# Attention in blocks of one token tile and sixteen heads, the first FFN layer of chunk 0 by token tiles, and the second chunk's transposes by DMA

## The chip, the cores and the metric

The kernel runs on one core of one Trainium2 chip. The metric is the device time of one execution in microseconds (us); lower is better. The time before is 501.07 us, the median of three runs (501.04 to 501.58).

## What is computed

One transformer layer over 2048 tokens of width 576: an attention with a compressive memory, then an FFN with a hidden width of 4608, each on a layer-normalized input and each with a residual.

```python
h = x + A(layernorm(x));  out = h + B(layernorm(h))

def A(x):                                  # 32 heads of 18, 4 segments of 512 tokens
    q, k, v = x @ wq, x @ wk, x @ wv
    M = z = 0;  g = sigmoid(beta)          # per head: M is 18 x 18, z is 18
    for s in range(4):
        p = softmax(qs @ ks.T * 18**-0.5 + causal_mask)
        a_mem = (phi(qs) @ M) / (phi(qs) @ z + 1e-6)   # phi(t) = t+1 if t>0 else exp(t)
        o_s = g * a_mem + (1 - g) * (p @ vs)
        M += phi(ks).T @ vs;  z += phi(ks).sum()
    return o @ wo

def B(x): return gelu(x @ w1 + b1) @ w2 + b2
```

## The kernel before

**Tiling.** A token tile is 128 tokens; a chunk is two tiles (256 tokens), so there are 16 tiles and 8 chunks (`NCH`); two chunks make a segment. All operands of matmuls are bf16. A group `g` is four heads (`G` = 8 groups): their Q and K lie transposed in `QTs` and `KTs`, one head in each quarter of the 128 partitions.

**An order planned at build.** Nothing is issued directly. Every piece of work is an `op` with an engine, a modelled duration, the keys it reads and writes, and a due time (`now` + a `SLACK` value). A small model of the engines runs through them: for ScalarE (ACT), VectorE (DVE), GpSimd (POOL) and the DMA-issuing SyncE (SP) the ready op with the earliest due time goes next (line 757); TensorE (PE) takes whichever generator ("stream") can go on, in an order of preference (lines 764 and 765). `transfer` and `begin` model one DMA queue by its rate. At the end (lines 792 to 794) all ops are issued in the order of their modelled start, which is then fixed. Each engine works its queue in that order, and waits where the chip is later than the model.

**The streams.** `stream_P(tl)` (two of them, one for each tile of a chunk) does layernorm, the transposes of the normalized tile, the Q/K/V projection (four pieces of 432 columns at lines 294 and 295), and the transposes of Q and K. For chunks below `TP` = 2 the transposes are matmuls into PSUM with copies out (lines 320 and 358, 401 and 404); from chunk 2 on they are DMA transposes on SP's queue (`dma_t`, line 130). It then makes phi(k) for the memory. `stream_M` sums phi(k)^T v (line 439). `stream_A` is the attention. `stream_B(tl)` is the output projection, the residual, the second layernorm and its transposes (matmuls for chunk 0 alone, `TB` = 1). `stream_F1` and `stream_F2` are the two FFN layers of a chunk.

**Attention.** A visit of `stream_A` is one group of four heads with up to two key tiles, for both query tiles of the chunk: `scores` puts 8 matmuls (line 482; four row groups of 32 side by side, 256 or 128 columns) into the four PSUM banks of `st4`, one exp on ScalarE takes them to `pt` (line 488; 384 or 512 columns in each bank), and an affine select on GpSimd masks each diagonal piece (line 492). `weighted` multiplies them with V (line 507, 128x19 matmuls into the PSUM bank `ox`). A chunk has 8 visits (even) or 16 (odd). The scores of a visit stand ahead of the weighted sums of the visit before it; at the end of a chunk the last sums follow with nothing ahead of them. After two groups, `finish` normalizes `ox` on VectorE (lines 547 to 560) for both tiles and eight heads; from chunk 2 on `memory_in` and `memory_mm` add the memory's part. The stream starts on a chunk when both of its tiles are projected (`done_P`), and `stream_B` when all visits of the chunk are done (`done_A`).

**FFN.** F1 of a chunk starts when both tiles have left `stream_B` (`done_B`): 9 weight groups of 512 hidden columns, each 4 x 5 matmuls of 256 columns (lines 294 and 295), with an eviction on VectorE for two of the four (line 703), and gelu on ScalarE in place over 18 hidden tiles at a time (line 711). The weight groups 0 to 4 of chunk 0 have buffers of their own (two, and three in the second hidden buffer, which is not used yet). Their loads 2 to 4 and those of W2 (`load_w2`, in the list `later`) are queued one at each attention visit. F2 (line 737) needs the gelu of the whole chunk.

**Filler.** As long as no F1 work has been issued, a TensorE that would stand idle multiplies the zeros of `pq` (line 775); the result is not read.

Of the kernel before, what the change touches and what calls it, by code (L numbers as in the profile page):

```python
# [16 lines left out]
def kernel(  # L17
# [447 lines left out]
    oxv = ox[:, 0:304].rearrange("p (u a b c) -> p u a b c", u=2, a=2, b=4)  # L465

    def scores(c, g, pieces, slot):
        s0 = c - c % 2
        placed = []
        off = 0  # L470
        for kt in pieces:
            lo = max(kt - 2 * (c % 2), 0)
            placed.append((kt, lo, off))
            off += (2 - lo) * P
        keys = [("QT", c % 2, 0), ("QT", c % 2, 1)] + [("KT", (s0 + kt // 2) % 3, kt % 2) for kt in pieces]
        sk = [("st", i) for i in range(4)]

        def go():
            for kt, lo, o in placed:
                for i in range(4):  # L480
                    rows = slice(32 * i, 32 * i + 32)
                    nc.tensor.matmul(out=st4[:, i, o:o + (2 - lo) * P],  # L482
                                     lhsT=KTs[(s0 + kt // 2) % 3][rows, g, (kt % 2) * P:(kt % 2 + 1) * P],
                                     rhs=QTs[c % 2][rows, g, lo * P:Q], start=True, stop=True, tile_position=(32 * i, 0))
# [2 lines left out]
        op("PE", 0.21 + off * MM, go, keys, sk)
        op("ACT", 0.18 + 4 * off * 0.00083, lambda: nc.scalar.activation(out=pt[:, :, 0:off], in_=st4[:, :, 0:off],  # L488
                                                                       func=ACT.Exp, scale=scale), sk, [("pt", slot)], slack=SLACK["exp"], table="exp")
        for kt, lo, o in placed:  # L490
            if kt >= 2 * (c % 2):
                op("POOL", 0.675, lambda o=o: nc.gpsimd.affine_select(  # L492
                    out=pt[:, :, o:o + P], in_=pt[:, :, o:o + P], pattern=[[0, 4], [1, P]], compare_op=ALU.is_ge,
                    fill=0.0, base=0, channel_multiplier=-1), (), [("pt", slot)], slack=SLACK["mask"])
        return placed

    def weighted(c, g, placed, slot):
        s0 = c - c % 2
        vk = [(v, (2 * s0 + kt) % 6, *j) for kt, _, _ in placed for v, *j in (("v", 0), ("v", 1), ("v1",))]

        def go():
            opens = g % 2 == 0 and placed[0][0] == 0
            for kt, lo, o in placed:
                for i in range(4):
                    for qt in range(lo, 2):
                        blk = o + (qt - lo) * P
                        nc.tensor.matmul(out=oxv[:, g % 2, qt, i, :], lhsT=pts[slot][:, i, blk:blk + P],  # L507
                                         rhs=v_augs[(2 * s0 + kt) % 6][:, 4 * g + i, :], start=opens, stop=False,
                                         skip_group_check=True)
                        opens = False  # L510

        n = sum(4 * (2 - lo) for _, lo, _ in placed)
        op("PE", n * 0.025, go, [("pt", slot)] + vk, ["ox"])

    def memory_in(c, g):
        q2 = QTs[c % 2][:, g:g + 2, :]
        qk = [("QT", c % 2, 0), ("QT", c % 2, 1)]
        e_g = ek[:].rearrange("p h d -> p (h d)")[:, 0:2 * Q].rearrange("p (u q) -> p u q", u=2)
        op("ACT", 0.63, lambda: nc.scalar.activation(out=e_g, in_=q2, func=ACT.Exp), qk, ["ek"], slack=SLACK["ek"], table="exp")
        op("POOL", 0.61, lambda: nc.gpsimd.tensor_scalar(out=pq[:], in0=q2, scalar1=BIG, scalar2=0.0, op0=ALU.min, op1=ALU.max),  # L520
           qk, ["pq"], slack=SLACK["relu"])
        op("DVE", 0.2, lambda: nc.vector.tensor_scalar(out=e_g, in0=e_g, scalar1=1.0, scalar2=None, op0=ALU.min), (), ["ek"], slack=SLACK["min"])  # L522
        op("POOL", 1.15, lambda: nc.gpsimd.tensor_tensor(out=pq[:], in0=e_g, in1=pq[:], op=ALU.add), ["ek"], ["pq"], slack=SLACK["add"])  # L523

    def memory_mm(c, g, b):
        j = (c // 2) % 2
        om = banks[b][:, 0:304].rearrange("p (u a b c) -> p u a b c", u=2, a=2, b=4)

        def go():
            for u in range(2):  # L530
                for qt in range(2):
                    nc.tensor.matmul(out=om[:, u, qt, :, :].rearrange("p i e -> p (i e)"), lhsT=pq[:, u, qt * P:(qt + 1) * P],
                                     rhs=MZ_blk[j][:, g + u, :], start=True, stop=True)
# [291 lines left out]
```

## Time and profile before

| | |
|---|---|
| Median of 3 runs | 501.07 us (501.04 to 501.58) |
| The profiled execution | 498.7 us |
| Span of its profile, core 0 | 497.0 us |
| Mean granted TensorE clock | 0.996 |
| TensorE busy | 480.1 us (97%) |
| ScalarE, VectorE, GpSimd busy | 292.2, 283.8, 206.6 us |
| DMA | 80.89 MB, mean 163 GB/s |

The span is one execution taken by the hardware profiler. Busy time counts each instruction from its start to its end; matmuls are pipelined, so their lengths overlap and the distance between two starts is what one costs. Lines are of the kernel's code. "PE L294 ... x4" in the timeline is four instructions merged; brackets give the idle time of the engine before it and what ended it.

### The profile page before, as it was taken

Reading aid. Unit: us, or ns where it says so; the run is one execution under the profiler, and the core shown is the slowest. Engines: PE = TensorE matmul, PEld = TensorE weight load, DVE = VectorE, ACT = ScalarE, POOL = GpSimd, SP = SyncE. Lnnn points to the kernel's source line nnn. Section 1 sums busy time; section 2 is a strip of 40 time slices with the busy share of each in tenths; the row PEclk is TensorE's granted clock in tenths of the full one; section 3 lists DMA queues with packets and bytes.
Section 4 is the critical chain, followed back from the end, with each engine's and each line's share of the span. In section 5 each row is a group of like instructions: output and inputs, shape, how many; then the busy total and the mean of one; then the engine's idle time right before and its main releaser. Section 6 shows DMA issues by size and latency. Waiting matters only on the chain.

```text
span 497.0 us, 13329 instructions
## 1 busy us (share of the span) xinstructions
PE 480.1 (97%) x5525; PEld 363.1 (73%) x5525; DVE 283.8 (57%) x696; ACT 292.2 (59%) x221; POOL 206.6 (42%) x291
## 2 busy tenths in 40 slices
PE   8999899798999999999999999999999999999997
PEld 5756578556577877766587787767887878878885
DVE  5868765487577534699456434876734443634411
ACT  3477868953557878657518687666357867122210
POOL 5565541279556331779331423596404242200000
PEclk9999999899999999999999999999999999999999
DMA  8985575549877453958977345777854445765411
GB/s 245 299 281 161 102 164 156 137 58 187 175 169 194 143 169 99 228 106 173 196 199 194 124 153 155 175 113 239 195 172 126 144 138 154 203 206 155 139 37 47
DMA packets 117340, 80.89 MB, mean 163 GB/s; under 512 B 56392, under 2 KB 115232, under 8 KB 117280
## 3 DMA queue, kind: packets, MB, share of 16 engines
q1 hardware_dynamic: 117248, 80.04, 62.3%
q8 instruction: 43, 0.70, 0.6%
q14 instruction: 17, 0.14, 0.1%
q0 software_dynamic: 32, 0.01, 0.1%
HBM read 60.10 MB, written 7.08 MB: 135 GB/s over the span
## 4 chain that ended last, share of the span: by engine, by line
PE 81%; DVE 7%; DMA 6%; ACT 2%; SPq 1%; issue 1%; POOL 0%; DVEq 0%; ACTq 0%
PE bank L294 34%; PE bank L737 23%; PE bank L295 8%; PE ox L507 6%; PE st L482 5%; PE ox L737 2%; DMA w1g<-in_B_w_dram 2%; DMA wqkv<-in_A_wk_dram 1%; DMA xT<-xn 1%; PE ox L294 1%; DVE xn L314 1%; DMA xT<-o_nat 1%; ACT hT L711 1%; DVE stats_p L301 1%; DVE r L550 1%
## 5 line engine op out<-in xcount | busy, mean ns | idle before, releaser
L488 ACT ACTIVATE pt<-st 128x2048 bf16<-128x2048 f32 (+1 forms) x96 | 153.0, 1594 | 99.8 <-PE st L482 98.6
L703 DVE CAST hT<-bank 128x512 bf16<-128x512 f32 x139 | 95.7, 689 | 104.3 <-PE bank L295 103.3
L737 PE MATMUL bank<-w_sb,hT 128*128 128x288 bf16 x1044 | 150.7, 287 | 3.0 <-ACT hT L711 3.0
L294 PE MATMUL bank<-xn2T,w1g 128*128 128x256 bf16 x1032 | 149.1, 272 | 0.4 <-DMA w1g<-in_B_w_dram 0.4
L737 PEld LDWEIGHTS <-hT 128*128 128x128 bf16 x1152 | 109.3, 98 | 31.8 <-ACT hT L711 3.3
L492 POOL TENSOR_SCALAR_AFFINE_SELECT pt<-pt 128x512 bf16<-128x512 bf16 x128 | 80.3, 652 | 97.7 <-ACT pt L488 97.6
L294 PEld LDWEIGHTS <-w1g 128*128 128x128 bf16 x1072 | 99.8, 97 | 20.4 <-issue 5.1
L711 ACT ACTIVATE hT<-hT 128x4608 bf16<-128x4608 bf16 (+1 forms) x22 | 65.9, 2996 | 46.0 <-DVE hT L703 45.9
L295 PE MATMUL bank<-xn2T,w1g 65*128 65x256 bf16 x258 | 70.7, 274 | 0.8 <-DMA w1g<-in_B_w_dram 0.8
L294 PE MATMUL bank<-wqkv,xT 128*128 128x432 bf16 x252 | 56.4, 345 | 2.8 <-DMA xT<-xn 2.6
L294 PEld LDWEIGHTS <-xT 128*128 128x128 bf16 x384 | 34.8, 98 | 27.2 <-DMA xT<-xn 3.0
L507 PEld LDWEIGHTS <-pt 128*128 128x128 bf16 x1280 | 43.9, 96 | 9.6 <-issue 6.0
L507 PE MATMUL ox<-v_aug,pt 128*128 128x19 bf16 x1280 | 47.0, 172 | 0.7 <-DVE o_nat L557 0.3
L523 POOL TENSOR_TENSOR pq<-ek,pq 128x512 bf16<-128x512 bf16 x24 | 27.9, 1163 | 27.2 <-DVE ek L522 27.0
L482 PE MATMUL st<-QT,KT 32*128 32x256 bf16 (+1 forms) x768 | 34.8, 255 | 0.7 <-ACT pt L488 0.6
L563 POOL TENSOR_TENSOR o_nat<-t,t 128x288 bf16<-128x288 f32 x24 | 19.4, 806 | 31.2 <-DVE t L560 31.1
L295 PEld LDWEIGHTS <-w1g 65*128 65x128 bf16 x268 | 26.1, 97 | 4.5 <-DMA w1g<-in_B_w_dram 1.4
L741 DVE TENSOR_TENSOR ot<-bank,hc 128x288 bf16<-128x288 f32 x29 | 13.2, 456 | 24.9 <-PE bank L737 21.3
L482 PEld LDWEIGHTS <-KT 32*128 32x128 bf16 x768 | 11.7, 92 | 18.9 <-issue 17.4
L376 ACT CAST qk_pad<-bank 128x432 bf16<-128x432 f32 x31 | 16.0, 520 | 14.4 <-PE bank L295 14.1
L645 POOL TENSOR_TENSOR h_t<-h_t,b_bc 128x576 f32<-128x576 f32 x16 | 20.5, 1279 | 7.1 <-DVE xn L314 7.1
L294 PE MATMUL bank<-wo_t,xT 128*128 128x288 bf16 x128 | 21.3, 293 | 1.9 <-DMA xT<-o_nat 0.9
(98 smaller groups left out, 476.6 us busy)
## 6 DMA issues: line engine op xcount, KB each, us to landing
w1g<-in_B_w_dram SPq DMA_DIRECT2D x67, 512.0 KB
w_sb<-in_B_w_dram SPq DMA_DIRECT2D x6, 864.0 KB
hd<-h_t SPq DMA_DIRECT2D x16, 288.0 KB
hc<-hd SPq DMA_DIRECT2D x32, 144.0 KB
w1g<-in_B_w_dram SPq DMA_DIRECT2D x67, 64.0 KB
x_b<-in_A_x_dram SPq DMA_DIRECT2D x18, 144.0 KB
hT<-in_B_w_dram SPq DMA_DIRECT2D x5, 512.0 KB
out_dram<-ot SPq DMA_DIRECT2D x16, 144.0 KB
```

The costliest lines, as they stand in the source:

```text
L294: nc.tensor.matmul(out=out_ap, lhsT=lhsT_of(slice(0, P), k), rhs=rhs_of(slice(0, P), k), start=(k == 0), stop=False)
L295: nc.tensor.matmul(out=out_ap, lhsT=lhsT_of(slice(0, KTAIL), 4), rhs=rhs_of(slice(0, KTAIL), 4), start=False, stop=True)
L482: nc.tensor.matmul(out=st4[:, i, o:o + (2 - lo) * P], lhsT=KTs[(s0 + kt // 2) % 3][rows, g, (kt % 2) * P:(kt % 2 + 1) * P], rhs=QTs[c % 2] ...
L488: op("ACT", 0.18 + 4 * off * 0.00083, lambda: nc.scalar.activation(out=pt[:, :, 0:off], in_=st4[:, :, 0:off], func=ACT.Exp, scale=scale), ...
L492: op("POOL", 0.675, lambda o=o: nc.gpsimd.affine_select(out=pt[:, :, o:o + P], in_=pt[:, :, o:o + P], pattern=[[0, 4], [1, P]], compare_op ...
L507: nc.tensor.matmul(out=oxv[:, g % 2, qt, i, :], lhsT=pts[slot][:, i, blk:blk + P], rhs=v_augs[(2 * s0 + kt) % 6][:, 4 * g + i, :], start=o ...
L523: op("POOL", 1.15, lambda: nc.gpsimd.tensor_tensor(out=pq[:], in0=e_g, in1=pq[:], op=ALU.add), ["ek"], ["pq"], slack=SLACK["add"])
L563: op("POOL", 0.7, lambda: nc.gpsimd.tensor_tensor(out=o_dst, in0=t1v, in1=t2v, op=ALU.add), ["t1", "t2"], ok, slack=SLACK["sum"])
L645: op("POOL", 1.36, lambda: nc.gpsimd.tensor_tensor(out=h_t[:], in0=h_t[:], in1=b2_bc[:], op=ALU.add), ["b2"], [("h", tl)], slack=SLACK["hb"])
L703: op("DVE", 0.684, lambda hT=hT, jp=jp, acc=acc: nc.vector.tensor_copy(out=hT[:, 2 * jp:2 * jp + 2, :], in_=acc), [b], [("hT", c % 2, jp)] ...
L711: op("ACT", (f1 - f0) * Q * 0.00083 + 0.18, lambda hT=hT, f0=f0, f1=f1: nc.scalar.activation(out=hT[:, f0:f1, :], in_=hT[:, f0:f1, :], fun ...
L737: nc.tensor.matmul(out=acc, lhsT=hT[:, q, tl * P:(tl + 1) * P], rhs=w2_sb[:, q, hs], start=(q == 0), stop=(q == NF - 1))
```

## The change

Attention goes in blocks of one query tile (`qt`) and sixteen heads (`gh`, four groups). The units of a block are its (group, key tile) pairs, 4, 8, 12 or 16 of them, and a visit is four units of 128 columns in each bank. The visits of all chunks form one list, so that the first scores of a chunk stand ahead of the last sums of the chunk before. A block may start when its own tile is projected (`half_P`); `stream_B` of a tile starts when the tile's two blocks are done (`half_A`). Where all four units are diagonal, the sums go in two parts of two units. For chunk 0 the weight groups 0 to 4 (`AHEAD`) of F1 go by token tiles, with matmuls of 128 columns, a tile as soon as it has left `stream_B`. `TP` falls from 2 to 1: chunk 1's transposes are DMAs. In the planner the due times are new throughout, chunk 0's `finish`, residual and second layernorm are due 8 us earlier (`head`), and an operation of GpSimd and some of VectorE (`port=True`) are modelled as longer while the other of the two is in one.

```diff
-    TP, TB = 2, 1
+    TP, TB = 1, 1
...
-    SLACK = dict(lnp=5, lnb=6.5, pow=4, apply=-8, ek_k=4, relu_k=9, min_k=0.5, add_k=10, mz=2.5, exp=-5, ek=9.5,
-                 relu=13.5, min=4.5, add=0, hb=27, gelu=17.5, finish=3.5, mem=-2, sum=-2, out=8, hd=17, xp=0.5, xb=10,
-                 t_x=34, t_q=19.5, t_k=34, t_o=23, t_h=14, w1=1.5, w2=16, hc=25.5, evict=0, qk=-3, ot=-7, mask=0,
-                 lead=1.5, balance=21)
+    SLACK = dict(head=8, lnp=16, lnb=2.5, pow=-0.5, apply=9, ek_k=47.5, relu_k=-8, min_k=4, add_k=15.5, mz=20,
+                 exp=12.5, ek=21.5, relu=33.5, min=13, add=30.5, hb=42, gelu=28.5, finish=0, mem=-0.5, sum=26.5,
+                 out=7.5, hd=29.5, xp=19.5, xb=20, t_x=23, t_q=11, t_k=26.5, t_o=17, t_h=24, w1=10, w2=32, hc=4.5,
+                 evict=-2, qk=4.5, ot=-6.5, mask=3.5, lead=1.5, balance=21)
...
+        if getattr(o, "port", False):
+            dur += max(0.0, port_until["POOL" if o.eng == "DVE" else "DVE"] - now)
+            port_until[o.eng] = now + dur
...
+    LATER, AHEAD = 0, 5
...
         def go():
-            for kt, lo, o in placed:
+            for n, (g, kt) in enumerate(units):
                 for i in range(4):
                     rows = slice(32 * i, 32 * i + 32)
-                    nc.tensor.matmul(out=st4[:, i, o:o + (2 - lo) * P],
-                                     lhsT=KTs[(s0 + kt // 2) % 3][rows, g, (kt % 2) * P:(kt % 2 + 1) * P],
-                                     rhs=QTs[c % 2][rows, g, lo * P:Q], start=True, stop=True, tile_position=(32 * i, 0))
+                    nc.tensor.matmul(out=st4[:, i, n * P:(n + 1) * P],
+                                     lhsT=KTs[(c - c % 2 + kt // 2) % 3][rows, g, (kt % 2) * P:(kt % 2 + 1) * P],
+                                     rhs=QTs[c % 2][rows, g, qt * P:(qt + 1) * P], start=True, stop=True, tile_position=(32 * i, 0))
...
+        op("ACT", 1.88, lambda: nc.scalar.activation(out=pt[:], in_=st4[:], func=ACT.Exp, scale=scale), sk,
+           [("pt", slot, n) for n in range(4)], slack=SLACK["exp"], table="exp")
...
     def stream_A():
-        n = 0
-        yield need(lambda: 0 in done_P and "ox" in bank_slots.free)
+        yield need(lambda: (0, 0) in half_P and "ox" in bank_slots.free)
...
+        visits = []
         for c in range(NCH):
...
+            for qt in range(2):
+                for gh in range(2):
+                    units = [(g, kt) for g in range(4 * gh, 4 * gh + 4) for kt in range(2 * (c % 2) + qt + 1)]
+                    visits += [(c, qt, gh, n == 0, n + 4 == len(units), units[n:n + 4]) for n in range(0, len(units), 4)]
+        back = []
+        for v in range(len(visits) + 1):
+            if v < len(visits):
+                c, qt, gh, first, last, units = visits[v]
+                seg = c // 2
+                yield need(lambda: (c, qt) in half_P and (c < 2 or (c - 2, qt) in half_B) and (seg == 0 or 2 * seg - 1 in done_M),
+                           None, score_keys(c, qt, units), [("st", i) for i in range(4)])
...
+                scores(c, qt, units, v % 3)
+                back.append((v % 3, visits[v]))
+            if v >= 1:
+                slot, (c, qt, gh, first, last, units) = back.pop(0)
+                own = 2 * (c % 2) + qt
+                parts = [(0, 1), (2, 3)] if sum(kt == own for _, kt in units) > 2 else [(0, 1, 2, 3)]
+                for part in parts:
+                    yield need(None, None, [("pt", slot, n) for n in part] + value_keys(c, units), ["ox"])
+                    weighted(c, units, part, slot, first and part[0] == 0)
...
+                if last:
+                    finish(c, qt, gh)
+                    if gh:
+                        half_A.add((c, qt))
...
-            yield need(lambda: c in done_A, xT_slots, idle=False)
+            yield need(lambda: (c, tl) in half_A, xT_slots, idle=False)
...
-            for jp in range(NF // 2):
+            if c == 0:
+                for tl in range(2):
+                    for n in range(AHEAD):
...
+                        yield need(lambda: (0, tl) in half_B, f_slots, xk[tl:tl + 1] + wk)
...
+                            op("PE", 5 * 0.0565, lambda acc=acc, a=a, wt=wt, tl=tl: mm5(
+                                acc[:, a, :], lambda r, k: wt[r, k, a * P:(a + 1) * P],
+                                lambda r, k: xn2T[0][r, k, tl * P:(tl + 1) * P]), xk[tl:tl + 1] + wk, [b])
...
+            for jp in range(0 if c else 2 * AHEAD, NF // 2):
```

`memory_in`, `memory_mm` and `finish` do the same arithmetic for one tile and sixteen heads at a time; for the first two chunks `finish` multiplies in one operation where it took two.

More of the change, by code (lines that the diff above doesn't have):

```diff
@@ L75 @@
     free_at = {"PE": 0.0, "SP": 0.0, "ACT": 0.0, "DVE": 0.0, "POOL": 0.0}
+    port_until = {"DVE": 0.0, "POOL": 0.0}
     queue = {e: [] for e in free_at}
@@ L79 @@
     class Op:
-        start, end, n = None, NEVER, None
+        start, end = None, NEVER
         def __init__(self, eng, dur, issue, preds, due, table=None, after=None):
@@ L109, in note, with op @@
             readers.setdefault(k, []).append(o)
-    def op(eng, dur, issue, rd=(), wr=(), slack=0.0, table=None):
+    def op(eng, dur, issue, rd=(), wr=(), slack=0.0, table=None, port=None):
         o = Op(eng, dur, issue, preds_of(rd, wr), now + slack, table)
+        o.port = eng == "POOL" if port is None else port
         ops.append(o)
@@ L463, in stream_M, with key_tiles @@
             done_M.add(c)
-    oxv = ox[:, 0:304].rearrange("p (u a b c) -> p u a b c", u=2, a=2, b=4)
-    def scores(c, g, pieces, slot):
+    oxv = ox[:, 0:304].rearrange("p (h e) -> p h e", e=E)
+    def key_tiles(c, kts):
         s0 = c - c % 2
[L469 to L475, printed above, removed]
+        return [(s0 + kt // 2, kt % 2) for kt in kts]
@@ L486, in scores @@
         pt = pts[slot]
[L487 to L494, printed above, removed]
@@ L495, in scores @@
-        return placed
-    def weighted(c, g, placed, slot):
+        op("PE", 0.43, go, score_keys(c, qt, units), sk)
+        op("ACT", 1.88, lambda: nc.scalar.activation(out=pt[:], in_=st4[:], func=ACT.Exp, scale=scale), sk,
+           [("pt", slot, n) for n in range(4)], slack=SLACK["exp"], table="exp")
+        for n, (g, kt) in enumerate(units):
+            if kt == own:
+                op("POOL", 0.65, lambda n=n: nc.gpsimd.affine_select(
+                    out=pt[:, :, n * P:(n + 1) * P], in_=pt[:, :, n * P:(n + 1) * P], pattern=[[0, 4], [1, P]],
+                    compare_op=ALU.is_ge, fill=0.0, base=0, channel_multiplier=-1), (), [("pt", slot, n)], slack=SLACK["mask"])
@@ L498, in weighted, with score_keys, value_keys @@
+    def score_keys(c, qt, units):
+        return [("QT", c % 2, qt)] + [("KT", kc % 3, t) for kc, t in key_tiles(c, sorted({kt for _, kt in units}))]
+    def value_keys(c, units):
+        return [(v, (2 * kc + t) % 6, *j) for kc, t in key_tiles(c, sorted({kt for _, kt in units}))
+                for v, *j in (("v", 0), ("v", 1), ("v1",))]
+    def weighted(c, units, part, slot, first):
         s0 = c - c % 2
-        vk = [(v, (2 * s0 + kt) % 6, *j) for kt, _, _ in placed for v, *j in (("v", 0), ("v", 1), ("v1",))]
@@ L501, in go @@
         def go():
-            opens = g % 2 == 0 and placed[0][0] == 0
-            for kt, lo, o in placed:
+            opens = first
+            for n in part:
+                g, kt = units[n]
                 for i in range(4):
[L505 to L520, printed above, removed]
+                    nc.tensor.matmul(out=oxv[:, 4 * (g % 4) + i, :], lhsT=pts[slot][:, i, n * P:(n + 1) * P],
+                                     rhs=v_augs[(2 * s0 + kt) % 6][:, 4 * g + i, :], start=opens, stop=False, skip_group_check=True)
@@ new lines, in go, with memory_in @@
+                    opens = False
+        op("PE", len(part) * 0.1, go, [("pt", slot, n) for n in part] + value_keys(c, units), ["ox"])
+    def memory_in(c, qt, gh):
+        q4 = QTs[c % 2][:, 4 * gh:4 * gh + 4, qt * P:(qt + 1) * P]
+        qk = [("QT", c % 2, qt)]
+        e_g = ek[:].rearrange("p h d -> p (h d)")[:, 0:4 * P].rearrange("p (g q) -> p g q", g=4)
+        op("ACT", 0.63, lambda: nc.scalar.activation(out=e_g, in_=q4, func=ACT.Exp), qk, ["ek"], slack=SLACK["ek"], table="exp")
+        op("POOL", 0.62, lambda: nc.gpsimd.tensor_scalar(out=pq[:], in0=q4, scalar1=BIG, scalar2=0.0, op0=ALU.min, op1=ALU.max),
@@ L521, in memory_in @@
            qk, ["pq"], slack=SLACK["relu"])
[L522 to L525 removed]
+        op("DVE", 0.2, lambda: nc.vector.tensor_scalar(out=e_g, in0=e_g, scalar1=1.0, scalar2=None, op0=ALU.min), (), ["ek"], slack=SLACK["min"],
+           port=True)
@@ L526, in memory_mm @@
+        op("POOL", 1.16, lambda: nc.gpsimd.tensor_tensor(out=pq[:], in0=e_g, in1=pq[:], op=ALU.add), ["ek"], ["pq"], slack=SLACK["add"])
+    def memory_mm(c, gh, b):
         j = (c // 2) % 2
-        om = banks[b][:, 0:304].rearrange("p (u a b c) -> p u a b c", u=2, a=2, b=4)
+        om = banks[b][:, 0:304].rearrange("p (u x) -> p u x", u=4)
         def go():
[L530 to L533, printed above, removed]
+            for u in range(4):
+                nc.tensor.matmul(out=om[:, u, :], lhsT=pq[:, u, :], rhs=MZ_blk[j][:, 4 * gh + u, :], start=True, stop=True)
```

124 lines of the change are left out of this document (60 added, 64 removed).

## The prediction

> **What bounds the kernel now.** I read the page first, then the same stretches twice (all work, then the filler matmuls of L775 alone), then TensorE's timeline.
>
> ```profile
> span 497.0 us, 13329 instructions
> PE 480.1 (97%) x5525; PEld 363.1 (73%) x5525; DVE 283.8 (57%) x696; ACT 292.2 (59%) x221; POOL 206.6 (42%) x291
> PE   8999899798999999999999999999999999999997
> PEclk9999999899999999999999999999999999999999
> PE 81%; DVE 7%; DMA 6%; ACT 2%; SPq 1%; issue 1%; POOL 0%; DVEq 0%; ACTq 0%
> ```
>
> TensorE is busy 97% and holds 81% of the chain that ended last; ScalarE, VectorE and GpSimd are busy 42 to 59%. So the time is TensorE's useful work plus the stretches in which it has none. The slices put the holes in the first quarter. By stage (columns: window, its length, busy us and instructions of PE, PEld, DVE, ACT, POOL, granted clock, DMA share, GB/s):
>
> ```profile
> 18.20:45.90 27.70, 26.54 (x385) 18.30 (x383) 21.60 (x58) 19.11 (x20) 17.88 (x25) 1.00 0.70 215
> 45.90:63.70 17.80, 15.82 (x216) 9.84 (x213) 13.34 (x38) 15.36 (x16) 9.86 (x13) 1.00 0.72 174
> 63.70:89.30 25.60, 25.60 (x357) 20.52 (x354) 15.66 (x30) 19.13 (x11) 6.75 (x10) 1.00 0.66 166
> 89.30:99.70 10.40, 7.37 (x75) 5.24 (x75) 4.10 (x14) 10.03 (x6) 3.58 (x7) 0.85 0.40 98
> 119.00:126.00 7.00, 4.39 (x50) 3.33 (x49) 2.24 (x5) 0.63 (x1) 5.27 (x6) 1.00 1.08 193
> 126.00:222.00 96.00, 95.57 (x1192) 72.30 (x1190) 59.32 (x152) 66.90 (x50) 48.43 (x67) 1.00 0.63 158
> 222.00:244.00 22.00, 20.51 (x217) 13.94 (x214) 16.11 (x39) 16.39 (x14) 16.15 (x22) 1.00 0.92 195
> 244.00:494.00 250.00, 249.35 (x2734) 196.28 (x2731) 123.25 (x278) 128.31 (x84) 73.52 (x99) 1.00 0.56 154
> ```
>
> The same stretches for L775 alone (matmuls whose result nobody reads, issued when TensorE has nothing to do before the first FFN work; columns PE, PEld, clock, DMA share, GB/s):
>
> ```profile
> 0.00:8.80 8.80, 5.92 (x37) 4.27 (x37) 1.00 0.77 210
> 18.20:45.90 27.70, 9.65 (x72) 6.42 (x72) 1.00 0.70 215
> ```
>
> So useful work is missing for 27.70 - 26.54 + 9.65 = 10.8 us in 18.2 to 45.9, for 17.80 - 15.82 = 2.0 in 45.9 to 63.7, for 3.0 in 89.3 to 99.7 plus 0.15 x 10.4 = 1.6 by the clock of 0.85 there, for 2.6 at 119 to 126 and 1.5 at 222 to 244: 21.5 us. From 126 on, outside that last hole, hardly 1.1 us is missing in 346. Before 8.8 TensorE waits for the first weights; the change loads them as before.
>
> TensorE's timeline around the steps (start, length, what):
>
> ```profile
> 17.79 0.61 PE L401 MATMUL bank<-ident,qk_pad 128*128 128x128 bf16 x8
> 18.23 1.80 PE L775 MATMUL bank<-pq 128*128 128x256 bf16 x15
> 19.97 0.34 PE L482 MATMUL st<-QT,KT 32*128 32x256 bf16 x8
> 20.25 1.81 PE L775 MATMUL bank<-pq 128*128 128x256 bf16 x15
> ...
> 41.91 0.46 PE L507 MATMUL ox<-v_aug,pt 128*128 128x19 bf16 x12
> 42.29 0.40 PE L482 MATMUL st<-QT,KT 32*128 32x256 bf16 x8
> 42.62 1.16 PE L775 MATMUL bank<-pq 128*128 128x256 bf16 x9
> ...
> 63.76 0.60 PE L294 MATMUL bank<-xn2T,w1g 128*128 128x256 bf16 x4
> ...
> 66.69 0.60 PE L294 MATMUL bank<-xn2T,w1g 128*128 128x256 bf16 x4
> 67.13 0.27 PE L295 MATMUL bank<-xn2T,w1g 65*128 65x256 bf16 x1
> 67.33 0.34 PE L482 MATMUL st<-QT,KT 32*128 32x256 bf16 x8
> ...
> 71.21 0.45 PE L507 MATMUL ox<-v_aug,pt 128*128 128x19 bf16 x12
> 71.51 0.60 PE L294 MATMUL bank<-xn2T,hT 128*128 128x256 bf16 x4
> ...
> 96.25 2.26 PE L737 MATMUL bank<-w_sb,hT 128*128 128x288 bf16 x10 [3.03 <-ACT hT L711]
> 125.20 0.90 PE L294 MATMUL bank<-wqkv,xT 128*128 128x432 bf16 x4 [2.61 <-DMA xT<-xn]
> ```
>
> Starts give the true prices, since the lengths include each matmul's tail: four matmuls of 256 columns take 67.13 - 66.69 = 0.44 (0.11 each), eight of 128 columns (L401) 18.23 - 17.79 = 0.44 (0.056 each), twelve weighted-sum matmuls 0.30 (0.025 each). FFN work begins at 63.76; until then only projections and attention can fill TensorE.
>
> **The change, part by part.**
>
> *Score visits.* Old: per two chunks 8 visits of 384 columns, 8 of 384 and 8 of 512: 64 and 32 in all. New: a block of one tile and four head groups has 4, 8, 12 or 16 units of 128 columns, so 6 visits for an even chunk and 14 for an odd one, 80 in all, each with 16 matmuls of 128 columns.
>
> ```profile
> L488 ACT ACTIVATE pt<-st 128x1536 bf16<-128x1536 f32 x64 | 92.9, 1452 | 55.6 <-PE st L482 55.3
> L488 ACT ACTIVATE pt<-st 128x2048 bf16<-128x2048 f32 x32 | 60.1, 1877 | 44.2 <-PE st L482 43.3 <-POOL pt L492 0.7
> L482 PEld LDWEIGHTS <-KT 32*128 32x128 bf16 x768 | 11.7, 92 | 18.9 <-issue 17.4
> L507 PEld LDWEIGHTS <-pt 128*128 128x128 bf16 x1280 | 43.9, 96 | 9.6 <-issue 6.0
> L492 POOL TENSOR_SCALAR_AFFINE_SELECT pt<-pt 128x512 bf16<-128x512 bf16 x128 | 80.3, 652 | 97.7 <-ACT pt L488 97.6
> ```
>
> A 384-column visit takes 20.25 - 19.97 = 0.28 from its first matmul to the next work, and before it TensorE stands from 67.13 + 0.11 to 67.33, 0.09: 0.37. A 512-column one takes 0.33 + 0.09 = 0.42. Four row groups run side by side, so 0.28 = 0.11 + 0.056 + a tail of 0.115. New visit: 4 x 0.056 + 0.115 + 0.09 = 0.43. Sum 80 x 0.43 - (64 x 0.37 + 32 x 0.42) = 34.4 - 37.1 = **-2.7 us** on TensorE. That takes the four weight loads of a step as hidden behind 56 ns of streaming; the trace has no such visit. If each step took the 0.11 of the 256-column ones, a visit would cost 0.645 and the sum would be +14.5. I take 0.43, since loads of 96 ns (L507) follow each other every 25 ns, so 92 ns is delay rather than spacing. The Trainium skill says otherwise ("TensorE: Matmul & The Clock Gate", LDWEIGHTS): a load takes its columns over 1.2 GHz, 32 rows as long as 128, which is 107 ns a step and 0.63 a visit; L507's 25 ns speaks against it for full-height loads, and no row here for short ones.
>
> ScalarE's exps go from 153.0 to 80 x 1.877 = 150.2; the 128 masks (0.652 us) and 1280 weighted sums stay. VectorE's and GpSimd's finishing work stays within 2 us. None of it sets the end at 42 to 59% busy; without that cover the exps would gain 2.8.
>
> *Second chunk's transposes.* 2 x (5 + 16) transposes leave TensorE: 42 x 0.056 = **-2.4 us**; two ScalarE copies and four VectorE copies go too, off the path. Added are six DMA transposes, a path of two in series (x, then Q and K) before chunk 1's scores.
>
> ```profile
> 27.61 0.45 SPq L677 DMA_DIRECT2D w_sb<-in_B_w_dram  x1
> 41.26 1.33 SPq L130 DMA_TRANSPOSE xT<-xn  x1
> ...
> 119.87 5.29 DMA xT<-xn
> ```
>
> SP issues nothing from 28.1 to 41.3, so 6 x 1.33 = 8 us of issuing fit, though SP keeps order: the W2 pieces and the later x tiles queue behind a transpose that waits for its layernorm, and F2 behind W2. A transpose took 5.3 us to land at 119.9 (DMA share 1.08). Two in series, with projection and copies between (some 4.5 us), give about 15 us; begun near 25, when the old kernel transposed this tile, Q and K of tile 2 land near 41 to 45. The old kernel's first chunk-1 scores start at 42.29 and need both tiles; the new ones need one. So chunk 1 starts about when it did, not earlier.
>
> *The new wait.* One list of visits runs over all chunks, and a visit's scores stand ahead of the sums of the visit before it. So the last sums of chunk 0 queue behind chunk 1's first scores, and finish, output projection and F1 of tile 1 wait with them: near 45, where the old one summed at 41.91.
>
> *First FFN layer by tiles.* 5 groups x 4 x 5 x 2 = 200 matmuls at 0.056 for 100 at 0.11: **+0.2 us**. The Trainium skill (same page, Back-to-back issue gap) has 81 ns for N=128 in a stream with weight loads; this would make it +5.2, and L401, which also loads weights for each of its matmuls, shows 56. What it buys is an earlier start: tile 0's attention is two visits from about 16 (its Q and K copies), and with the first exp and eight masks in a row it is done near 16 + 0.4 + 1.9 + 8 x 0.652 = 23.5. The old path from the last sum to F1 (41.91 to 63.76) carried two tiles; half of its 21.9 puts tile 0's F1 near 35, 28 us earlier, w1 groups 0 to 4 being loaded first.
>
> *What fills 18.2 to 45.9.* Six visits 6 x (0.43 + 16 x 0.025) = 5.0, projections of chunk 1 as before 8 x 0.92 = 7.4, F1 of tile 0 100 x 0.056 = 5.6, output path of tile 0 about 1.8, memory sums 0.5: 20.3 of 27.7, so 7.4 missing for 10.8: **-3.4 us** (ends 0 and -10.8). In 45.9 to 63.7: 7 visits 5.8, output path 1.8, F1 of tile 1 5.6 and the rest of F1 16 x 0.55 = 8.8, chunk 2's projections 7.4: 29 for 17.8, so the 2.0 shrinks to 0.5: **-1.5** (0 to -2.0).
>
> *The stall at 93.* F1 of chunk 0 was used up there, F2 waited for the gelu (3.03 us), and the clock fell. F1 now ends some 20 us sooner, so the gelu is past and F2's 17 us of work lie ready. I take **-4.1** of 4.6 (ends 0 and -4.6). At 119 and 222 I take nothing: all due times are new, each engine's order is rewritten, and as many misses may come as go (plus or minus 4, the size of the two).
>
> Sum: -2.7 - 2.4 + 0.2 - 3.4 - 1.5 - 4.1 = -13.9. The profiled execution took 498.7 (span 497.0 and 1.7 around it), so 484.8; against the median 501.07, which lies 2.4 above it, **487.2**.
>
> **The rivals.**
> 1. *The head stays as empty.* Chunk 1's Q and K land late in the DMA queue, tile 1 waits with them, the fill of 18 to 64 gains nothing. For it: DMA share 0.70 to 0.72 there. Against: tile 0's F1 needs neither. Time 487.2 + 4.9 = 492.
> 2. *The holes only move.* F1, spent earlier, leaves a later gap of the old size: all three gains of waiting go, leaving the 4.9 of work: 496.2. For it: the holes in the trace are the planner's misses. Against: TensorE's backlog grows.
> 3. *Slower: short weight loads are not hidden.* If the next step's loads in the same rows do not keep up with 56 ns of streaming, each of 320 steps stretches. Without the score term the sum is -11.2; it is used up when 80 x (4s + 0.205) = 37.1 + 11.2, at a step of s = 0.10. At the 0.11 of the old steps: 501.07 - 11.2 + 14.5 = 504.4; at 92 + 56 ns, load after stream, 517. For it: L482's loads last 92 ns. Against: L507's overlap. By the skill's 107 ns it would be 503.4.
>
> **How the numbers follow.** Forecast 0.44; rival 1 0.22; rival 2 0.12; rival 3 0.12; still faster, with the whole head filled (479), 0.05; new misses that eat all gain 0.05 (half within 0.2%, half slower). About 0.2% is what a measurement of this kernel can tell from no change. Faster 0.83, same 0.03, slower 0.14. The range takes in rivals 1 and 2 with the planner's 4 us, and leaves out the slow end and the best: 480 to 500.
>
> **What would show it.** First scores near 16 to 17 and F1 matmuls of 128 columns near 35; filler beyond 18.2 under 7 us; score visits whose four steps are 0.06 apart; no clock of 0.85 near 93. I am wrong if the steps are 0.10 or more apart, if tile 1's last sums come after 50, or if holes of over 3 us stand between 60 and 130.

## The result and the profile after

The changed kernel takes 483.68 us (median of four runs, 482.71 to 486.99) against 501.32 for the kernel before in the same comparison (four runs, 501.04 to 502.31). The ratio of the means is 0.966, with a 95% interval of 0.961 to 0.971; run once more beside other kernels it stood at 0.971 (0.967 to 0.974). It is faster, and 3.5 us below the forecast 487.2.

The page of the changed kernel, with the lines that answer to those of before:

```profile
span 481.0 us, 14391 instructions
PE 470.9 (98%) x6074; PEld 368.8 (77%) x6074; DVE 283.1 (59%) x684; ACT 288.8 (60%) x204; POOL 208.0 (43%) x291
PEclk9999999999999999999999999999999999999999
PE 87%; DMA 7%; DVE 2%; SPq 1%; ACT 1%; issue 1%; POOL 0%; DVEq 0%; ACTq 0%
```

The span fell by 16.0 us and TensorE's busy time by 9.2; its share of the chain rose from 81% to 87%. The other engines have the work they had. The stages, in the windows of the prediction (the last one ends 3 us before the span does, as before):

```profile
8.80:18.20 9.40, 8.78 (x78) 5.18 (x78) 3.79 (x10) 3.93 (x7) 2.32 (x3) 1.00 1.04 296
18.20:45.90 27.70, 26.11 (x431) 18.95 (x428) 21.49 (x53) 21.50 (x20) 19.93 (x30) 1.00 0.90 216
45.90:63.70 17.80, 16.14 (x346) 12.97 (x343) 15.08 (x38) 13.25 (x10) 9.64 (x14) 1.00 1.17 269
63.70:89.30 25.60, 25.35 (x406) 20.34 (x404) 18.55 (x42) 21.72 (x14) 10.01 (x14) 1.00 0.97 215
89.30:99.70 10.40, 9.64 (x113) 6.36 (x114) 7.38 (x20) 9.88 (x8) 7.57 (x12) 1.00 0.35 75
99.70:119.00 19.30, 19.12 (x231) 14.62 (x228) 13.67 (x39) 6.61 (x8) 12.06 (x16) 1.00 0.92 209
119.00:126.00 7.00, 7.00 (x84) 3.92 (x82) 4.32 (x12) 5.17 (x7) 6.31 (x9) 1.00 0.27 64
126.00:222.00 96.00, 96.00 (x1307) 75.77 (x1300) 61.64 (x153) 70.78 (x45) 50.51 (x69) 1.00 0.66 166
222.00:244.00 22.00, 21.95 (x275) 16.94 (x274) 17.18 (x42) 7.56 (x9) 11.48 (x14) 1.00 1.03 198
244.00:478.00 234.00, 233.32 (x2785) 188.09 (x2782) 113.65 (x255) 126.42 (x79) 70.88 (x95) 1.00 0.57 153
```

The filler matmuls alone (now at L805) in two of these windows (columns PE, PEld, clock, DMA share, GB/s):

```profile
8.80:18.20 9.40, 0.75 (x6) 0.45 (x5) 1.00 1.04 296
18.20:45.90 27.70, 5.48 (x41) 3.69 (x41) 1.00 0.90 216
```

Useful work is missing for 27.70 - 26.11 + 5.48 = 7.1 us in 18.2 to 45.9 (10.8 before), 1.7 in the next stage (2.0), 0.8 at 89.3 to 99.7 (4.6 with the clock), 0.0 at 119 to 126 (2.6), 0.05 at 222 to 244 (1.5) and 1.1 in the rest (1.3). That is 10.7 against 22.8: 12.1 us of holes are filled. The stretch up to 18.2 goes the other way. From 8.8 on 0.6 is idle and 0.75 filler, where the kernel before had

```profile
8.80:18.20 9.40, 9.24 (x75) 5.65 (x73) 3.96 (x10) 3.58 (x7) 1.63 (x3) 1.00 1.09 322
```

with no filler, and before 8.8 useful work is 0.5 us less; 1.7 us are lost there in all. So 16.0 - 12.1 + 1.7 = 5.6 us are left for work that TensorE no longer has, where the prediction had 4.9.

TensorE's timeline at the places the prediction named:

```profile
17.01 0.40 PE L489 MATMUL st<-QT,KT 32*128 32x128 bf16 x16
17.34 0.90 PE L300 MATMUL bank<-wqkv,xT 128*128 128x432 bf16 x4
...
23.68 0.90 PE L300 MATMUL bank<-wqkv,xT 128*128 128x432 bf16 x4 [1.04 <-DMA xT<-xn]
...
27.07 0.56 PE L518 MATMUL ox<-v_aug,pt 128*128 128x19 bf16 x16
...
36.50 0.54 PE L489 MATMUL st<-QT,KT 32*128 32x128 bf16 x16
...
39.07 0.55 PE L518 MATMUL ox<-v_aug,pt 128*128 128x19 bf16 x16
...
43.12 0.40 PE L300 MATMUL bank<-xn2T,w1g 128*128 128x128 bf16 x4
...
58.35 0.39 PE L300 MATMUL bank<-xn2T,hT 128*128 128x128 bf16 x4
58.58 0.22 PE L301 MATMUL bank<-xn2T,hT 65*128 65x128 bf16 x1
58.64 0.39 PE L300 MATMUL bank<-xn2T,hT 128*128 128x128 bf16 x4
...
62.26 0.23 PE L300 MATMUL bank<-xn2T,w1g 128*128 128x128 bf16 x1 [1.16 <-issue]
```

First scores stand at 17.01, the first of chunk 1 at 36.50, the last sums of chunk 0 come 2.6 us behind them at 39.07, and FFN work begins at 43.12 where it began at 63.76. And SP's queue in the changed kernel:

```profile
19.94 1.33 SPq L132 DMA_TRANSPOSE xT<-xn  x1
...
27.65 1.25 SPq L132 DMA_TRANSPOSE QT<-qk_pad  x1
...
31.54 1.24 SPq L132 DMA_TRANSPOSE KT<-qk_pad  x1
...
34.23 2.46 SPq L686 DMA_DIRECT2D w_sb<-in_B_w_dram  x3
```

The transposes of tile 2 go out ahead of the W2 pieces (L686), of which the kernel before had issued four by 28.

### The profile page after: what moved, and what is told of

The parts are those of the page before. It is cut to its first block, busy times and chain, and to the rows that moved or that the text cites. A ratio compares the mean times of both kernels' runs of the same rounds, so it can differ in the third digit from the quotient of the medians.

```text
span 481.0 us, 14391 instructions
## 1 busy us (share of the span) xinstructions
PE 470.9 (98%) x6074; PEld 368.8 (77%) x6074; DVE 283.1 (59%) x684; ACT 288.8 (60%) x204; POOL 208.0 (43%) x291
## 4 chain that ended last, share of the span: by engine, by line
PE 87%; DMA 7%; DVE 2%; SPq 1%; ACT 1%; issue 1%; POOL 0%; DVEq 0%; ACTq 0%
PE bank L300 36%; PE bank L767 25%; PE bank L301 9%; PE ox L518 6%; PE st L489 5%; PE ox L767 3%; DMA xT<-o_nat 2%; DMA wqkv<-in_A_wv_dram 2%; DMA xT<-xn 2%; PE ox L300 1%; DMA w1g<-in_B_w_dram 1%; DMA x_p<-in_A_x_dram 1%; ACT pt L495 1%; PE bank L447 1%; PE bank L541 1%
## 5 line engine op out<-in xcount | busy, mean ns | idle before, releaser
L495 ACT ACTIVATE pt<-st 128x2048 bf16<-128x2048 f32 x80 | 150.2, 1877 | 74.5 <-PE st L489 70.6
L300 PE MATMUL bank<-xn2T,w1g 128*128 128x256 bf16 (+1 forms) x1056 | 149.2, 269 | 1.3 <-issue 1.2
L733 DVE CAST hT<-bank 128x512 bf16<-128x512 f32 x128 | 88.1, 689 | 85.3 <-PE bank L301 83.2
L300 PEld LDWEIGHTS <-w1g 128*128 128x128 bf16 x1104 | 101.2, 97 | 19.0 <-issue 1.3
L741 ACT ACTIVATE hT<-hT 128x4608 bf16<-128x4608 bf16 (+5 forms) x23 | 66.1, 2875 | 52.9 <-DVE hT L733 52.7
L301 PE MATMUL bank<-xn2T,w1g 65*128 65x256 bf16 (+1 forms) x264 | 71.5, 271 | 0.0
L518 PE MATMUL ox<-v_aug,pt 128*128 128x19 bf16 x1280 | 45.2, 172 | 0.0
L489 PE MATMUL st<-QT,KT 32*128 32x128 bf16 x1280 | 32.3, 217 | 0.1
L771 DVE TENSOR_TENSOR ot<-bank,hc 128x288 bf16<-128x288 f32 x29 | 13.2, 456 | 29.8 <-PE bank L767 29.7
L489 PEld LDWEIGHTS <-KT 32*128 32x128 bf16 x1280 | 18.6, 92 | 13.9 <-issue 11.4
L301 PE MATMUL bank<-wqkv,xT 65*128 65x432 bf16 x63 | 21.9, 348 | 0.0
```

The costliest lines, as they stand in the source:

```text
L300: nc.tensor.matmul(out=out_ap, lhsT=lhsT_of(slice(0, P), k), rhs=rhs_of(slice(0, P), k), start=(k == 0), stop=False)
L301: nc.tensor.matmul(out=out_ap, lhsT=lhsT_of(slice(0, KTAIL), 4), rhs=rhs_of(slice(0, KTAIL), 4), start=False, stop=True)
L489: nc.tensor.matmul(out=st4[:, i, n * P:(n + 1) * P], lhsT=KTs[(c - c % 2 + kt // 2) % 3][rows, g, (kt % 2) * P:(kt % 2 + 1) * P], rhs=QTs[ ...
L495: op("ACT", 1.88, lambda: nc.scalar.activation(out=pt[:], in_=st4[:], func=ACT.Exp, scale=scale), sk, [("pt", slot, n) for n in range(4)], ...
L518: nc.tensor.matmul(out=oxv[:, 4 * (g % 4) + i, :], lhsT=pts[slot][:, i, n * P:(n + 1) * P], rhs=v_augs[(2 * s0 + kt) % 6][:, 4 * g + i, :] ...
L733: op("DVE", 0.684, lambda hT=hT, jp=jp, acc=acc: nc.vector.tensor_copy(out=hT[:, 2 * jp:2 * jp + 2, :], in_=acc), [b], [("hT", c % 2, jp)] ...
```

## The experiments

The question was where the 16 us come from: from the structure (visits of four units, tiles released one by one, F1 by tiles), from the DMA transposes, or from the due times, which are all new. In the table, "missing" is a window's length less TensorE's busy time, plus the filler in it, plus what the granted clock below 1.00 costs; "rest" ends 3 us before the span.

| kernel | median us | ratio to before (95%) | missing 18.2-64 | 64-130 | 130-rest |
|---|---|---|---|---|---|
| before | 501.32 | 1 | 12.8 | 7.7 | 2.6 |
| changed | 483.68 | 0.966 (0.961-0.971) | 8.7 | 1.2 | 0.7 |
| changed, again (a_again) | 486.27 | 0.971 (0.967-0.974) | 8.4 | 2.4 | 2.1 |
| a_ahead0 | 499.36 | 0.997 (0.994-1.001) | 9.6 | 5.1 | 11.1 |
| a_tp2 | 487.83 | 0.974 (0.969-0.980) | 5.9 | 2.6 | 2.9 |
| a_oldslack | 501.87 | 1.001 (0.997-1.005) | 9.2 | 5.9 | 11.2 |
| a_gate | 508.76 | 1.018 (1.011-1.025) | 13.2 | 7.8 | 11.9 |
| a_ahead0_r | 492.16 | 0.986 (0.982-0.991) | 12.3 | 5.3 | 2.7 |
| a_gate_r | 490.42 | 0.984 (0.980-0.988) | 16.8 | 1.8 | 1.0 |
| a_noport_r | 489.83 | 0.983 (0.979-0.987) | 7.8 | 4.9 | 3.1 |
| b_port_r | 498.66 | 1.001 (0.997-1.005) | 13.1 | 7.4 | 1.9 |
| a_tp2_r | 485.55 | 0.970 (0.966-0.974) | 3.6 | 4.3 | 3.0 |
| b_tp1_r | 500.75 | 1.000 (0.998-1.003) | 25.0 | 1.5 | 3.8 |
| a_c0gel_r | 483.34 | 0.964 (0.960-0.968) | 9.7 | 1.1 | 1.6 |

The level of the kernel before differed between the comparisons (498.4 to 501.3), so kernels are compared by their ratios. Expectations in us were made on the level of the first one: at 501.3 a ratio of 0.983 is 493 us, 0.986 is 494 and 0.997 is 500.

### One part undone, the table of due times left as it is

**F1 of chunk 0 by whole chunks.**

```diff
-    LATER, AHEAD = 0, 5
+    LATER, AHEAD = 0, 0
```

> The changed kernel with one thing undone: chunk 0's first FFN layer goes by whole chunks again (AHEAD 0). Theory: the gain is 4.9 us of TensorE work and the rest is holes filled by work that is ready earlier. Then without F1 by tiles nothing but projections and attention can fill TensorE until both tiles are through the output path, near 55, and the 1.7 us missing between 45.9 and 63.7 grows by 3 to 5: 487 to 489, against 483.7. Rival (the new due times make the gain, not the early start): no more than 1.5 us slower.

It took 499.36: nearly the whole gain was gone, about three times the largest loss that the theory gave. But the loss is not where it should be: 18.2 to 64 has 9.6 us missing against 8.7, while 11.1 are missing after 130 (7.4 idle, the rest by the clock of 0.99), where chunk 0 is long done:

```profile
130.00:495.00 365.00, 357.58 (x4373) 281.67 (x4361) 195.67 (x455) 207.00 (x135) 133.27 (x178) 0.99 0.63 157
```

**Chunk 1's transposes on TensorE.**

```diff
-    TP, TB = 1, 1
+    TP, TB = 2, 1
```

> The changed kernel with chunk 1's transposes on TensorE again (TP 2). Theory: 42 matmuls of 128 columns come back at 0.056, 2.4 us, and nothing else, since SP and the DMA queue have room: 485 to 487. Rival (the DMA path of two transposes in series holds chunk 1 back): chunk 1 starts before 36 and the time falls below 483.

487.83, just above the theory's range, at a ratio 0.008 above the changed kernel's first one and 0.003 above its second. The rival's condition came true, its time did not: chunk 1's first scores start before 36, at

```profile
34.82 0.40 PE L489 MATMUL st<-QT,KT 32*128 32x128 bf16 x16
```

so the path of the DMAs does hold chunk 1 back, by some 1.7 us. The head has less missing (5.9 for 8.7), the later stages more.

**The due times of the kernel before.**

```diff
-    SLACK = dict(head=8, lnp=16, lnb=2.5, pow=-0.5, apply=9, ...)
+    SLACK = dict(head=0, lnp=5, lnb=6.5, pow=4, apply=-8, ...)
```

> The changed kernel with the due times of the kernel before (head 0). Theory: the structure carries the work and the early start, so at least the 4.9 us of work and the 3.7 of the head stay: at most 493, and likely 487 to 490 with one or two planner holes back. Rival (the due times make the gain): 495 or more, with holes of over 2 us between 60 and 250.

501.87: nothing was left of the gain, though the work is that of the changed kernel. The first theory fell here, and the rival had the number. Where it went (TensorE's windows; columns as above):

```profile
64.00:130.00 66.00, 62.09 (x900) 48.45 (x898) 36.47 (x89) 44.38 (x31) 31.38 (x44) 0.97 0.66 141
130.00:498.60 368.60, 357.39 (x4404) 282.11 (x4402) 206.25 (x471) 207.96 (x138) 136.58 (x184) 1.00 0.63 158
```

368.60 - 357.39 = 11.2 us stand empty after 130, where both the kernel before (2.6) and the changed one (0.7) are nearly full. TensorE's largest waits after 130 have many causes (line waited for: us in total, times, longest):

```profile
PE bank L300 <- DMA w1g<-in_B_w_dram: 2.1, 3, 1.0
PE bank L301 <- DMA w1g<-in_B_b_dram: 1.8, 2, 1.4
PE bank L300 <- DMA xT<-o_nat: 1.7, 3, 1.1
PE bank L300 <- DVE hT L733: 1.3, 1, 1.3
```

None of them is long. The kernel's longest single wait lies earlier: the gelu stall of the kernel before (F2 waiting for the gelu near 93) is back in the new structure, 3.28 us at 95.44 (shown further below), and with it the rival's sign, a hole of over 2 us.

**Everything released by whole chunks.**

```diff
-        yield need(lambda: (0, 0) in half_P and "ox" in bank_slots.free)
+        yield need(lambda: 0 in done_P and "ox" in bank_slots.free)
...
-                yield need(lambda: (c, qt) in half_P and (c < 2 or (c - 2, qt) in half_B) and (seg == 0 or 2 * seg - 1 in done_M),
+                yield need(lambda: c in done_P and (c < 2 or c - 2 in done_B) and (seg == 0 or 2 * seg - 1 in done_M),
...
-            yield need(lambda: (c, tl) in half_A, xT_slots, idle=False)
+            yield need(lambda: c in done_A, xT_slots, idle=False)
```

> The changed kernel, but attention of a chunk waits for both of its tiles and the output path for the whole chunk, as before; the visits of four units, F1 by tiles and the DMA transposes stay. Theory: the 4.9 us of work stay and the early start goes: 487 to 492, with filler between 18 and 46 back near 9 us. Rival (the early start buys nothing, as the planner finds other fill): within 1.5 us of 483.7.

508.76, worse than the kernel before. The filler in 18.2 to 45.9 is back as expected (11.8 us), but 11.9 us are missing after 130 as well. Two edits of the first 60 us (a_ahead0 and a_gate) each cost some 11 us after 130: the order of the whole kernel hangs on the table. A part undone under a table fitted to something else measures the misfit as much as the part.

### Each structure with its own due times

So the next kernels had the table fitted to their own structure, all in the same way: the SLACK values are changed at random, and the table is kept for which the kernel's own planner ends soonest (some 1400 to 1600 changes each; four searches of some 1150 for b_tp1_r, 650 changes for a_c0gel_r). For the changed kernel and for the old one the same search found planned ends less than 0.1% earlier, so these two stand as they are; that figure is the planner's, and no run timed those tables. How long the changed kernel's own table had been searched is not known.

**F1 by whole chunks, fitted.**

```diff
-    LATER, AHEAD = 0, 5
+    LATER, AHEAD = 0, 0
-    SLACK = dict(head=8, lnp=16, lnb=2.5, ...)
+    SLACK = dict(head=18, lnp=6.5, lnb=16.5, ...)
```

> The changed kernel with F1 of chunk 0 by whole chunks (AHEAD 0), and the table of due times fitted to this structure: some 1400 random changes of the SLACK table, and the one kept for which the kernel's own planner ends soonest. With the old table the same kernel stood at 499.4. Theory A (a plan is only as good as its due times; what the structure is worth shows when each structure has its own): most of the 16 us come back, 486 to 490, with holes of over 1 us between 60 and 260 gone, and 2 to 5 us stay lost, near 45 to 64. Theory B (without early F1 the holes are forced): 495 or more.

492.16 (0.986, or 494 at the first level), between the theories and nearer to B: by the ratios the fit gave back 5 to 6 us of the gain that was lost. The holes after 130 went (2.7), and those in the head stayed:

```profile
18.20:64.00 45.80, 43.32 (x723) 31.60 (x720) 33.77 (x91) 35.43 (x31) 29.96 (x43) 1.00 0.93 221
64.00:130.00 66.00, 60.66 (x764) 44.44 (x763) 45.82 (x111) 40.55 (x33) 32.60 (x46) 1.00 0.75 170
```

with filler (L802 here) in the first of them:

```profile
18.20:64.00 45.80, 9.78 (x70) 6.10 (x70) 1.00 0.93 221
```

2.5 + 9.8 = 12.3 us missing to 64 and 5.3 to 130, where the kernel before had 12.8 and 7.7. Without F1 by tiles the head is as empty as it was, and the stretch after it nearly so. But here TensorE waits between 64 and 130 for transposed tiles above all (3.7 us), and only 1.1 us for the gelu.

**Released by whole chunks, fitted.** The edits of a_gate, and

```diff
-    SLACK = dict(head=8, lnp=16, lnb=2.5, ...)
+    SLACK = dict(head=1, lnp=31.5, lnb=28, ...)
```

> The changed kernel with attention and the output path released by whole chunks, and its due times fitted in the same way (with the old table: 508.8). Theory A: 488 to 494; more than with AHEAD 0, since filler comes back in 18 to 46 (11.8 us there with the old table, 5.5 in the changed kernel). Theory B: 500 or more.

490.42 (0.984, or 493 at the first level), in theory A's range, from 508.76 with the changed kernel's table; it lost no more than a_ahead0_r, which theory A had expected of it. Here all of the loss is in the head, which has more missing (16.8) than in the kernel before (12.8); the filler of L802 in 18.2 to 64:

```profile
18.20:64.00 45.80, 11.55 (x95) 8.84 (x95) 0.96 0.92 220
```

**No model of VectorE and GpSimd in each other's way, fitted.**

```diff
-        if getattr(o, "port", False):
+        if False:
-    SLACK = dict(head=8, lnp=16, lnb=2.5, ...)
+    SLACK = dict(head=40, lnp=12.5, lnb=36, ...)
```

> The changed kernel with the planner's model of VectorE and GpSimd in each other's way left out, and its due times fitted in the same way. The instructions are the same, only their order differs. Theory A: an order planned without these delays meets them on the chip, so small waits come back: 484 to 490. If the model carried the gain: 492 or more.

489.83 (0.983): the same work, 1.2 to 1.7% slower than the changed kernel. At the first level that is 493, outside theory A and just inside the other. What is missing lies later than the head, 2.2 us of it a wait for the gelu:

```profile
64.00:130.00 66.00, 63.04 (x870) 46.36 (x869) 45.18 (x115) 47.49 (x36) 38.14 (x53) 0.97 0.81 157
130.00:483.90 353.90, 350.81 (x4305) 278.96 (x4302) 196.05 (x441) 197.67 (x133) 129.76 (x174) 1.00 0.63 160
```

How much of this loss is the model and how much the luck of one search is open.

**The old structure with the new model and a fitted table.** The planner's port model is put into the kernel before at the same operations, and

```diff
-    SLACK = dict(lnp=5, lnb=6.5, pow=4, ...)
+    SLACK = dict(lnp=11, lnb=4.5, pow=-14, ...)
```

> The kernel before with nothing changed in its work: the planner's model of VectorE and GpSimd is added and the due times are fitted to it in the same way. Theory A (the old structure is the limit, not its table): 494 to 501. Theory B (the new table and the better model make the gain, whatever the structure): 490 or less.

498.66 against 498.40 beside it, a ratio of 1.001, as theory A had it: model and fit are worth nothing to the old structure. It has 1.9 us missing after 130, and 13.1 and 7.4 before (2.25 of it filler after 64, since F1 starts at 68.41). Its holes are in the head, and it has the gelu stall too, 3.0 us at 99.91.

### The transposes by DMA

**TensorE's transposes in the changed kernel, fitted**, the edit of a_tp2 and

```diff
-    SLACK = dict(head=8, lnp=16, lnb=2.5, ...)
+    SLACK = dict(head=3.5, lnp=12.5, lnb=-8, ...)
```

> The changed kernel with chunk 1's transposes on TensorE (TP 2) and due times fitted to that. Theory A: with the old table this was 487.8 at a ratio of 0.974, of which 2.4 us are the 42 matmuls; fitted, only these stay: a ratio of 0.968 to 0.974, 1 to 3 us over the changed kernel. If the transposes by DMA carried more than their matmuls: over 4 us.

485.55 (0.970), beside 486.27 (0.971) for the changed kernel: in theory A's range, but no difference to the kernel beside it. Its filler (L802):

```profile
18.20:64.00 45.80, 1.30 (x9) 0.80 (x9) 1.00 0.75 207
```

1.3 us instead of 5.5. In the changed kernel the chain that ended last goes twice through a DMA transpose of x in the head, and in its second execution (a_again) TensorE also waits for that of K:

```profile
19.94 3.69 DMA xT<-xn
...
32.89 4.29 DMA xT<-xn
```

```profile
38.23 0.29 PE L489 MATMUL st<-QT,KT 32*128 32x128 bf16 x8 [0.77 <-DMA KT<-qk_pad]
```

The chain of a_tp2_r has none of these before 46. So the 2.4 us of matmuls that the DMAs take off TensorE come back in the head as waiting, and more (8.7 us missing against 3.6); in the later stages a_tp2_r has more missing (7.3 us against 1.9 and 4.5 in the two executions), which is its own order.

**The transposes alone in the old structure, fitted.**

```diff
-    TP, TB = 2, 1
+    TP, TB = 1, 1
-    SLACK = dict(lnp=5, lnb=6.5, pow=4, ...)
+    SLACK = dict(lnp=16, lnb=39.5, pow=-33, ...)
```

> The kernel before with one part of the change alone: chunk 1's transposes by DMA (TP 1), with due times fitted to that. 2.4 us of TensorE work go, but in the old structure chunk 1's attention waits for both tiles and there is no FFN work to fill the path of the DMAs, so filler takes their place. Theory A: no gain, a ratio of 0.997 to 1.010. Rival (work taken from TensorE is time taken from the end): 0.995.

500.75 (1.000 +- 0.003), as theory A had it. Work left TensorE, and filler (L772) took its place:

```profile
18.20:64.00 45.80, 40.10 (x553) 27.53 (x552) 28.44 (x85) 29.21 (x27) 24.13 (x35) 0.93 0.88 214
```

```profile
18.20:64.00 45.80, 16.05 (x116) 10.85 (x114) 0.93 0.88 214
```

16.1 us for 9.7, and the clock was 0.93 in this stretch. From 64 to 130 it has 1.5 us missing for 7.7, with the old structure and F1 starting only at 72.13: the gelu stall is gone there too.

### The same kernel again, and another order for it

The changed kernel, unchanged:

> The changed kernel, unchanged, beside the others on one chip. Its ratio to the kernel before was 0.966 (0.961 to 0.971); the same is expected, whatever the level of this chip.

It came at 0.971, at the edge of that interval. Its profiled execution has a span of 484.6 where the first had 481.0, with the same order of instructions:

```profile
64.00:130.00 66.00, 63.56 (x857) 46.91 (x855) 46.93 (x118) 45.30 (x37) 37.87 (x52) 1.00 0.79 172
130.00:481.60 351.60, 349.50 (x4329) 279.17 (x4326) 190.46 (x441) 202.93 (x130) 131.57 (x175) 1.00 0.64 158
```

2.4 and 2.1 us missing where the first had 1.2 and 0.7: waits of about 1 us or less that come and go between executions of one program. The first comparison's four executions alone had spans of 481.0 to 485.0.

**Gelu of chunk 0 in smaller pieces, fitted.**

```diff
-                if f1 - f0 >= (6 if alone else 18) or f1 == NF:
+                if f1 - f0 >= (6 if alone else (6 if c == 0 else 18)) or f1 == NF:
-    SLACK = dict(head=8, lnp=16, lnb=2.5, ...)
+    SLACK = dict(head=7, lnp=9, lnb=12, ...)
```

> The changed kernel with chunk 0's gelu in pieces of 6 hidden tiles instead of 18, and due times fitted to it: another order that the planner holds to be as short. Theory A: TensorE has no hole at the gelu any more, so nothing is to be won there: within 4 us of the changed kernel run beside it, the spread showing what orders of equal plan differ by on the chip. If the gelu still held something up: 2 us or more faster.

483.34 (0.964, 0.960 to 0.968), four runs of 482.50 to 484.66 beside four of the changed kernel of 485.95 to 486.83. In this comparison it is faster by 2.9 us or 0.6%, so both expectations were met, which leaves the question where it was. Whether the smaller gelu or merely another order did it is not settled: its span of 482.9 lies between those of two executions of the changed kernel.

## Why the prediction was right, and where it was not

- **What bounds it.** Right. Filled stretches (12.1) less what the first 18.2 us lost (1.7) leave 5.6 us for saved work, against a forecast of 4.9. The loss in the first 18.2 us, where the prediction expected no change, is a miss.
- **Score visits, -2.7.** Right: 17.34 - 17.01 = 0.33 from the first score to the next work, as four steps of 0.056 and the tail of 0.115 gave (0.34). Rival 3 is refuted, since a step of 0.10 would make 0.5. By the length of a load in the Trainium skill ("TensorE: Matmul & The Clock Gate", LDWEIGHTS), taken as the step of 107 ns, it would have been 0.54 (an estimate). The trace has loads of 92 ns and no such step, so a load's length is not the distance between two, for loads of 32 rows too. No run undoes this part alone.
- **F1 by tiles, +0.2.** Nearly right: five matmuls of 128 columns in 58.64 - 58.35 = 0.29, or 0.058 each, which makes +0.6. The Trainium skill's 81 ns (same page, Back-to-back issue gap) does not hold here.
- **Second chunk's transposes, -2.4.** The step failed as a gain. The path of DMAs was estimated well: from the first issue at 19.94 to chunk 1's scores at 36.50 it took 16.6 us (estimate 15). But nothing was put down for the waiting that this path brings in the head. b_tp1_r gains nothing within 0.3%, where 2.4 us would be 0.5%. For the changed structure no gain was seen either (a_tp2_r), but there 2.4 us lie within what one fit may be off by.
- **Q and K near 41 to 45, F1 of tile 0 near 35.** Both wrong, in opposite directions. The path began at 19.9, not 25, so chunk 1's scores came at 36.50; the last sums of chunk 0 did queue behind them as foreseen, at 39.07 and so 2.8 us sooner than before, not later. Tile 0 needed 16 us from its last sums (27.07) to F1 (43.12), not 11. The errors cancelled: of the 5.6 us of F1 in the sum for 18.2 to 45.9 only some 1.2 stood there, and three visits of chunk 1 took their place. That 7.1 us were missing, where the sum had 7.4, is luck.
- **45.9 to 63.7.** 1.7 missing, not 0.5; 1.16 of it is one wait for "issue", whose cause the profile does not tell.
- **The stall at 93, -4.1.** Right in size (3.8 of 4.6 gone, clock 1.00), but not by the mechanism given, an earlier F1. The first F1 matmuls of a_gate_r and of b_tp1_r start later than before (63.76), and neither kernel waits for the gelu between 60 and 130:

```profile
65.84 0.39 PE L297 MATMUL bank<-xn2T,w1g 128*128 128x128 bf16 x4
```

```profile
72.13 0.60 PE L291 MATMUL bank<-xn2T,w1g 128*128 128x256 bf16 x4
```

a_oldslack and a_noport_r start F1 at 46.06 and 42.54, about as early as the changed kernel, and wait as F2 begins:

```profile
95.44 4.78 PE L767 MATMUL bank<-w_sb,hT 128*128 128x288 bf16 x24 [3.28 <-ACT hT L741]
```

```profile
91.67 2.15 PE L764 MATMUL bank<-w_sb,hT 128*128 128x288 bf16 x10 [2.25 <-ACT hT L738]
```

So an early F1 is neither needed nor enough. With the same instructions the table alone decides (a_oldslack against the changed kernel), and that the term had the size is luck.

- **The holes at 119 and 222, taken as nothing, within 4.** This is the mis-sized term: they gave 4.1, the end of that band, and explain most of why the time came out below 487.2.
- **Due times.** The largest miss in reasoning. They were a footnote of plus or minus 4, and they decide whether the rest is gained: the changed structure under the old table (a_oldslack) gains nothing, rival 2 and more. The structure under its own table gains 15 to 17; the old structure under a new one (b_port_r) gains nothing. Neither half is the cause alone: the structure gives work to put into the head, the fitted order keeps the rest of the kernel full.
- **The early start.** Undone in one way or the other and fitted, it costs 1.3 to 2.1% (0.986 and 0.984 against 0.966 and 0.971), 6 to 10 us; the prediction had 4.9 for the head and 4.1 for the stall. In the head a_ahead0_r has 3.6 us more missing than the changed kernel and a_gate_r 8.1. The two ways are not to be added, since both put F1 off.

What stays open: each variant has one fitted table from a random search, so 1% between two fitted kernels may be the search, and a longer search behind the changed kernel's table would make every undone part look dearer. What the single parts of the structure are worth is therefore known only roughly.

## What to carry to other kernels

When a kernel's order comes from a planner with tuned due times, structure and table are one thing: an edit measured under the other's table shows the misfit, so fit the table to each variant before comparing. Price a change against the bounding engine as work removed plus holes filled, stage by stage, and ask of each hole what work would be ready to fill it. Work that is taken off a full engine gains nothing if the path it is moved to makes that engine wait in the same stage. And where a term comes out in size, look for a variant that lacks the supposed cause: two here lost the wait for the gelu without an earlier F1.
